# Reordering the prologue of a causal-convolution kernel and giving its last products one block shape

## The chip, the cores and the metric

The kernel runs on one core of a Trainium2 chip. Times are device microseconds (us) of one execution. The profile is one further execution taken by the hardware profiler; its span is about 2 us shorter than the timed number. An execution would count as slow if it took over 1.5% more than the fastest of the same kernel.

In the profile PE is TensorE (matrix products and transposes), PEld its weight load, DVE is VectorE, ACT is ScalarE, POOL is GpSimd and SP is SyncE, which here only issues DMA transfers (SPq is its queue). L727 is line 727 of that kernel's own source file; the changed kernel's file is one line shorter, so L1024 before is L1023 after, and so on.

## The reference

A causal convolution over time (15 taps, 2 tokens apart), a gate, and an output product. x is 2 x 16000 tokens of 144 channels in bfloat16, w is 15 x 144 x 288, w_o is 144 x 144.

```python
def reference(x, w, w_o):
    B, T, D = x.shape
    K = w.shape[0]                      # 15 taps
    dil = 2
    pad = (K - 1) * dil                 # 28
    xp = jnp.pad(x, ((0, 0), (pad, 0), (0, 0)))
    h = jnp.einsum('btc,cd->btd', xp[:, pad:pad + T, :], w[0])
    for i in range(1, K):
        off = pad - i * dil
        h = h + jnp.einsum('btc,cd->btd', xp[:, off:off + T, :], w[i])
    f, g = h[..., :D], h[..., D:]       # (copies cut)
    return (jnp.tanh(f) * _sigmoid(g)) @ w_o
```

## The kernel before

The 32000 tokens are cut into 128 segments of 250, one for each partition. A tile holds one token of every segment, and eight tiles make an "oct". TensorE writes its results to PSUM (PS in the profile), where the program uses eight banks, 0 to 7, and VectorE or ScalarE copies them out (an *eviction*; the two XB evictions of 128x512 together took 1.01 us on VectorE before the change). The program multiplies with the channels on partitions, so every tile is transposed: in the prologue by TensorE itself, later by DMA (XA<-STA in the profile; STA is a staging copy made by VectorE). 128 of the 144 channels are in XA; the other 16, of eight tiles at a time, are in XB.

The first 10 tokens of each segment (the *direct* tiles, k = 0 to 9) are computed plainly: 15 matmuls against the weights WA, tap by tap, and two against WB for the 16 leftover channels. Tap i of tile e reads tile e - 2i, so taps 12 to 14 read the oldest tiles and taps 0 to 3 the newest. The other 240 tokens use a scheme that shares products between tokens. It saves matmuls and costs VectorE work: sums of weights (WC, WS, WT, WV, WD) and differences of tiles (V, DU, DD, GX, GU, GV, GD, BE, BF).

The order of instructions on each engine is fixed when the program is built, by the kernel's own list scheduler. It takes each operation's inputs, its scheduled duration (`dur`) and its `prio`; a `floating` operation may be moved past others on its engine. So a small change to one operation can shift the whole static order.

The prologue, with cuts ("..."):

```python
wa_pieces = [(0, 4), (4, 8), (8, 12), (12, 15)]       # taps of w, loaded in this order, between x's pieces
pro_pieces = [(0, 14), (14, 22), (22, E0), (E0, EP)]  # tiles of x: the oldest first
...
for o in range(-4, 1):                                # input transposes on TensorE (L565)
    b = (o + 4) % 4                                   # PSUM banks 0 to 3
    eng = "act" if o in (-3, -1, 0) else "dve"        # who copies them out of PSUM (L574)
    ...
warm(16)                                              # small matmuls that keep TensorE busy (L541)
...
for o, tiles, bb in ((-1, range(E0 - 4, E0), 7), (0, range(E0, E0 + 8), 5)):   # XB: banks 7 and 5
    ...                                               # 12 transposes (L602)
    g.add("dve", lambda v, ...: v.tensor_copy(XB[...], PSb[...]), ...)         # eviction on VectorE (L606)
...
for b in range(6, 8):                                 # one 288-wide matmul into bank 6, one into bank 7 (L1071)
    g.add("pe", [lambda t: t.matmul(bank(b), lhsT=ID[:], rhs=WARM[:], start=True, ...)], ...)

def direct(k, b, pi, t0, t1, after=None):             # taps t0 to t1 of direct tile k (L727)
    e = H + k
    g.add("pe", region(b, [XA tile e - 2 * i for i in range(t0, t1)], [WA[:, i, :] ...], start=(t0 == 0)),
          floating=k >= KF, prio=2 if k >= KF else 1, ...)        # KF = 6
for pi, (t0, t1) in enumerate(wa_pieces):             # taps 0 to 3 of six tiles, then 4 to 7, ...
    for k in range(6):
        direct(k, db[k], pi, t0, t1)
```

Here `start=True` marks the first matmul of a sum in the program; the later ones are meant to add to it.

The end. The last unit's odd tiles are not transposed by DMA but in four "end pairs": 144 channels are split in 128 + 16, so a 128x128 transpose alternates with a 128x16 one, and a product over 128 rows with one over 16:

```python
def ship_pair(o0, o1, dl):
    ...
    for i in range(2):
        fns.append(transpose(PSb[:, ...],    Z[:, zs[i], dl*D : dl*D+128]))        # L772, 128x128
        fns.append(transpose(PSb[0:DB, ...], Z[:, zs[i], dl*D+128 : dl*D+D]))      # L773, 128x16
    ...
    for i in range(2):
        fns.append(matmul(lhsT=zt(q, 128*i, 128), rhs=WOR[:, 0, :], start=(i == 0)))           # L780
        fns.append(matmul(lhsT=zt(q, 256+128*i, 128)[0:DB, :], rhs=WOR[0:DB, 1, :], start=False))  # L782
    ...                                                                            # ScalarE eviction L786, then stores
```

Of the kernel before, what the change touches and what calls it, by code (L numbers as in the profile page):

```python
# [327 lines left out]
def _conv_wavenet_kernel(nc, x, w, w_o, out):  # L328
# [39 lines left out]
    KF = 6  # L368
    LAG = 2
    SPREAD = 12  # L370
# [3 lines left out]
    with contextlib.ExitStack() as st:  # L374
# [25 lines left out]
        WARM = sb("WARM", [NP, N2], BF16)  # L400
# [94 lines left out]
        for pi, (e0, e1) in enumerate(pro_pieces):  # L495
            if pi:
                t0, t1 = wa_pieces[pi - 1]
                g.add("sp", ld_w(t0, t1), w=[("WA", pi - 1)], dur=0.55, dma="wa", nbytes=(t1 - t0) * 128 * N2 * 2)
            if e0 >= H:
                g.add("sp", ld_x(flat(Xp[:, e0:e1, :]), 0, NP, e0, e1), w=[("Xp", pi, 0), ("Xp", pi, 1)], dur=0.45, dma="xp", nbytes=NP * (e1 - e0) * D * 2)  # L500
                continue
            g.add("sp", ld_x(flat(Xp[1:1 + n16, e0:e1, :]), 1, 1 + n16, e0, e1), w=[("Xp", pi, 0)], dur=0.45, dma="xp", nbytes=n16 * (e1 - e0) * D * 2)
            g.add("sp", ld_x(flat(Xp[1 + n16:NP, e0:e1, :]), 1 + n16, NP, e0, e1), w=[("Xp", pi, 1)], dur=0.45, dma="xp", nbytes=15 * (e1 - e0) * D * 2)
        g.add("act", lambda e: e.dma_start(flat(Xp[0:1, 0:H, :]), bass.AP(x_t, 0, [[L * D, 1], [1, H * D]])), w=[("Xp", 0, 2)], dur=0.5, dma="xp", nbytes=8064)
        g.add("act", lambda e: e.dma_start(flat(Xp[0:1, H:E0, :]), bass.AP(x_t, 0, [[L * D, 1], [1, KD * D]])), w=[("Xp", 2, 2)], dur=0.5, dma="xp", nbytes=576)
        t0, t1 = wa_pieces[3]
        wa_op = g.add("sp", ld_w(t0, t1), w=[("WA", 3)], dur=0.55, dma="wa", nbytes=(t1 - t0) * 128 * N2 * 2)
# [11 lines left out]
        g.add("pool", lambda p: p.memset(WARM[:], 0.0), w=["WARM"], dur=0.3)  # L519
# [36 lines left out]
        for pi in range(4):  # L556
            e0, e1 = pro_pieces[pi]
            for o in range(-4, 1):
# [3 lines left out]
                b = (o + 4) % 4  # L562
# [6 lines left out]
                eng = "act" if o in (-3, -1, 0) else "dve"  # L569
# [7 lines left out]
            warm(16)  # L577
# [20 lines left out]
        for o, tiles, bb in ((-1, range(E0 - 4, E0), 7), (0, range(E0, E0 + 8), 5)):  # L598
            fns = []
            for e in tiles:  # L600
# [5 lines left out]
            g.add("dve", lambda v, o=o, i0=i0, bb=bb: v.tensor_copy(XB[:, bslot(o), i0:8, :].rearrange("p a b -> p (a b)"), PSb[:, bb * 1024 + 128 * i0:bb * 1024 + 1024]),  # L606
                  r=[bk], w=[("XB", bslot(o))], frees=[bk], dur=0.335 if o < 0 else 0.6)
# [156 lines left out]
        def ship_pair(o0, o1, dl):  # L764
# [6 lines left out]
            for i in range(2):  # L771
                fns.append(lambda t, i=i: t.transpose(PSb[:, pa.b * 1024 + 128 * i:pa.b * 1024 + 128 * i + 128], Z[:, zs[i], dl * D:dl * D + 128], ID[:]))  # L772
                fns.append(lambda t, i=i: t.transpose(PSb[0:DB, pb.b * 1024 + 128 * i:pb.b * 1024 + 128 * i + 128], Z[:, zs[i], dl * D + 128:dl * D + D], ID[:]))  # L773
            g.add("pe", fns, r=[("Z", zs[0], dl), ("Z", zs[1], dl), "ID"], alloc=[pa, pb], dur=0.24, floating=True)
            g.add("dve", lambda v: v.tensor_copy(zt(q, 0, 256), PSb[:, pa.b * 1024:pa.b * 1024 + 256]), r=[pa], w=[("ZTL", q, 0), ("Xr", 0)], frees=[pa], dur=0.21, prio=0)
            g.add("act", lambda a: a.activation(zt(q, 256, 256)[0:DB, :], PSb[0:DB, pb.b * 1024:pb.b * 1024 + 256], ACT.Copy), r=[pb], w=[("ZTL", q, 1)], frees=[pb], dur=0.29, prio=0)
            bo = _Bank()
            fns = []
            for i in range(2):
                fns.append(lambda t, i=i: t.matmul(PS[:, bo.b * 512 + i * D:bo.b * 512 + i * D + D], lhsT=zt(q, 128 * i, 128), rhs=WOR[:, 0, :],  # L780
                                                   start=(i == 0), stop=True, skip_group_check=True))
                fns.append(lambda t, i=i: t.matmul(PS[:, bo.b * 512 + i * D:bo.b * 512 + i * D + D], lhsT=zt(q, 256 + 128 * i, 128)[0:DB, :], rhs=WOR[0:DB, 1, :],  # L782
                                                   start=False, stop=True, skip_group_check=True))
# [274 lines left out]
        def direct(k, b, pi, t0, t1, after=None):  # L1058
            e = H + k
            g.add("pe", region(b, [(lambda e_=e - DIL * i: xa_tile(e_)) for i in range(t0, t1)], [(lambda i_=i: WA[:, i_, :]) for i in range(t0, t1)], t0 == 0),  # L1060
                  r=[("XA", aslot(o)) for o in sorted(set(oct_of(e - DIL * i)[0] for i in range(t0, t1)))] + [("WA", pi)], dur=(t1 - t0) * MM, floating=k >= KF, prio=2 if k >= KF else 1, soft=(after,), **({"alloc": [b.bk]} if t0 == 0 and k % 2 == 0 else {"w": [b.bk]}))

# [6 lines left out]
        for b in range(6, 8):  # L1069
            bk = _Bank(b)  # L1070
            g.add("pe", [lambda t, bk=bk: t.matmul(bank(bk.b), lhsT=ID[:], rhs=WARM[:], start=True, stop=True, skip_group_check=True)],  # L1071
                  r=["ID", "WARM"], alloc=[bk], frees=[bk], dur=MM)
# [7 lines left out]
        for pi, (t0, t1) in enumerate(wa_pieces):  # L1080
# [8 lines left out]
        def direct_parts(k):  # L1089
            out = [lambda pi=pi, t0=t0, t1=t1: direct(k, db[k], pi, t0, t1, fin[0] if k >= 8 and t0 == 0 else None) for pi, (t0, t1) in enumerate(wa_pieces)]  # L1090
# [90 lines left out]
        pattern = [(x.rstrip("+"), x.count("+")) for x in PATTERN.split()]  # L1181
# [8 lines left out]
        for t in range(-reach, NUN):  # L1190
# [3 lines left out]
            for name, off in pattern:  # L1194
# [36 lines left out]
        dorder = [x for x, _ in pattern if x[0] == "D"]  # L1231
# [91 lines left out]
```

## Time and profile before

Median 333.14 us (three runs). The span of the profile is 331.2 us.

| engine | busy, of a span of 331.2 us | in the steady part |
|---|---|---|
| TensorE | 323.0 us (98%) | 50.00 of every 50 us |
| VectorE | 302.6 us (91%) | 49.3 of 50 |
| ScalarE | 259.4 us (78%) | 42.9 of 50 |

From the page: the busy times, and the chain of waits (followed back from the last instruction, shares of the span by engine).

```profile
PE 323.0 (98%) x2736; PEld 249.4 (75%) x2736; DVE 302.6 (91%) x662; ACT 259.4 (78%) x626; POOL 17.2 (5%) x30
...
PE 93%; DVE 5%; ACT 1%; issue 1%; POOL 0%; POOLq 0%
```

The table by stretches of the same kernel. Its columns are the stretch and its length, then busy time and number of instructions of PE, PEld, DVE, ACT and POOL, then the granted clock (the share of TensorE's full clock), DMA share and GB/s.

```profile
5.80:14.70 8.90, 7.40 (x119) 6.88 (x116) 7.79 (x27) 3.78 (x6) 6.13 (x11) 1.00 0.88 251
14.70:27.50 12.80, 12.79 (x105) 10.22 (x106) 12.38 (x31) 4.28 (x10) 5.88 (x11) 1.00 0.93 175
35.00:45.00 10.00, 9.68 (x80) 7.50 (x79) 8.19 (x19) 5.65 (x16) 0.00 (x0) 1.00 1.07 205
105.00:155.00 50.00, 50.00 (x421) 38.44 (x419) 49.30 (x105) 42.90 (x106) 0.00 (x0) 1.00 0.70 146
```

TensorE has no gap from 65 to 305 us. The change does not touch that part, so whatever it gains must come before 65 us or after 305 us. The start in the timeline (start, duration, engine, line, operation; in brackets the idle time before it and who ended it):

```profile
14.25 1.01 DVE L606 COPY XB<-PS 128x512 bf16<-128x512 bf16 x2
14.71 0.30 PE L1071 MATMUL PS<-WARM,ID 128*128 128x288 bf16 x1 [1.51 <-DVE XB L606]
14.85 11.19 PE L727 MATMUL PS<-WA,XA 128*128 128x288 bf16 x90
25.87 1.63 PE L727 MATMUL PS<-WB,XB 128*128 128x288 bf16 x12
42.19 1.57 DVE L1024 TENSOR_TENSOR PS<-PS,Xp 128x576 f32<-128x576 f32 x2 [1.78 <-ACT UX L960]
```

The first real matmul (L727) comes at 14.85 us. Until then TensorE only transposes and warms up, and its last wait, 1.51 us, is for VectorE's copy of XB. The direct block ends at 25.87 + 1.63 = 27.50 us. At 42.19 VectorE has waited 1.78 us for ScalarE's copy UX of a matmul result, so there TensorE was what VectorE waited for.

The end, lines of TensorE and SyncE in the timeline (and ScalarE's last eviction):

```profile
320.05 0.22 PE L772 MATMUL PS<-ID,Z 128*128 128x128 bf16 x1
320.20 0.22 PE L773 MATMUL PS<-ID,Z 128*16 128x128 bf16 x1
320.35 0.23 PE L772 MATMUL PS<-ID,Z 128*128 128x128 bf16 x1
...
320.67 0.67 PE L863 MATMUL PS<-WOR,ZT 128*128 128x144 bf16 x8
...
324.61 1.42 SPq L808 DMA_DIRECT2D out_dram<-OS  x2
327.04 0.35 SPq L851 DMA_DIRECT2D out_dram<-OS  x1
327.43 0.42 SPq L799 DMA_DIRECT2D out_dram<-OS  x1
327.70 0.41 ACT L786 ACTIVATE OS<-PS 128x288 bf16<-128x288 f32 x1 [0.28 <-PE PS L782]
327.90 1.32 SPq L808 DMA_DIRECT2D out_dram<-OS  x2
```

Transposes that alternate in shape start 0.15 to 0.16 us apart. Eight projections of one shape take 0.67 us together. SyncE issues its last four stores from 327.04 to 329.22, with 0.05 us between them, after a pause of 1.01 us. The last eviction is done at 328.11.

### The profile page before, as it was taken

To read this page: it belongs to the slowest core of one execution; us is meant where nothing else is said; L and a number is where in the kernel's file an instruction comes from. 1 tells how busy PE (TensorE), PEld (TensorE's weight loads), DVE (VectorE), ACT (ScalarE), POOL (GpSimd) and SP (SyncE) were. 2 spreads that over 40 slices of the span, in tenths; PEclk is the share of its full clock that TensorE was granted. 3 is DMA by queue.
4 is the path that set the end of the run, shared out by engine and by line. 5 is a ranking of instruction groups with operands and counts; after the bars stand their busy time and mean duration, and the time that the engine had idled before them with its cause. 6 is when DMAs were issued, how large, how long until landed. Compare 5 with 4: busy or idle time off the path is not lost.

```text
span 331.2 us, 7123 instructions
## 1 busy us (share of the span) xinstructions
PE 323.0 (98%) x2736; PEld 249.4 (75%) x2736; DVE 302.6 (91%) x662; ACT 259.4 (78%) x626; POOL 17.2 (5%) x30
## 2 busy tenths in 40 slices
PE   7899999999999999999999999999999999999995
PEld 7787867777777777777777777777777777777773
DVE  1999889999999999999999999999999999895682
ACT  3327577979798897979798897979889797787754
POOL 8740000000000000000000000000000000000000
PEclk9999999999999999999999999999999999999997
DMA  8889942928759392956839394874919194411443
GB/s 213 265 124 210 218 121 43 191 84 169 174 99 206 81 207 100 182 158 126 218 63 194 117 177 135 146 200 93 248 38 200 38 154 117 97 48 38 107 109 107
DMA packets 112509, 46.46 MB, mean 140 GB/s; under 512 B 103822, under 2 KB 106303, under 8 KB 112477
## 3 DMA queue, kind: packets, MB, share of 16 engines
q1 hardware_dynamic: 111961, 45.68, 64.6%
q8 instruction: 21, 0.34, 0.4%
q0 software_dynamic: 512, 0.33, 0.4%
q14 instruction: 11, 0.09, 0.1%
q10 hardware_dynamic: 4, 0.01, 0.0%
HBM read 11.82 MB, written 9.22 MB: 64 GB/s over the span
## 4 chain that ended last, share of the span: by engine, by line
PE 93%; DVE 5%; ACT 1%; issue 1%; POOL 0%; POOLq 0%
PE PS L727 81%; PE PS L832 8%; DVE Xp L1012 2%; PE PS L541 1%; DVE WC L616 1%; DVE V L673 1%; DVE PS L1033 0%; PE PS L782 0%; PE PS L863 0%; PE PS L780 0%; PE PS L773 0%; DVE XA L574 0%; PE PS L772 0%; DVE PS L1024 0%; DVE Z L756 0%
## 5 line engine op out<-in xcount | busy, mean ns | idle before, releaser
L1012 DVE TENSOR_TENSOR Xp<-PS,UX 128x576 f32<-128x576 f32 x90 | 65.2, 752 | 7.0 <-PE PS L727 6.4
L1024 DVE TENSOR_TENSOR PS<-PS,Xp 128x576 f32<-128x576 f32 x90 | 68.2, 758 | 3.6 <-ACT UX L960 1.8
L727 PE MATMUL PS<-WA,GD 128*128 128x288 bf16 x360 | 69.8, 286 | 0.3 <-DVE PS L1024 0.3
L748 ACT ACTIVATE TS<-PS 128x288 f16<-128x288 f32 x125 | 51.4, 411 | 14.7 <-PE PS L727 10.0
L891 ACT ACTIVATE PS<-PS 128x288 f32<-128x288 f32 x120 | 45.4, 401 | 17.5 <-PE PS L727 17.5
L751 ACT ACTIVATE TS<-PS 128x288 f16<-128x288 f32 x125 | 50.7, 405 | 0.0
L960 ACT ACTIVATE UX<-PS 128x576 f32<-128x576 f32 x60 | 39.0, 651 | 14.7 <-PE PS L727 13.4
L727 PE MATMUL PS<-WS,GU 128*128 128x288 bf16 x210 | 44.1, 286 | 0.0
L655 ACT ACTIVATE STB<-XBc 128x512 bf16<-128x512 bf16 x60 | 35.9, 630 | 10.0 <-DVE V L673 5.6
L840 ACT ACTIVATE OS<-PS 128x432 bf16<-128x432 f32 (+1 forms) x88 | 42.4, 488 | 0.5
L832 PE MATMUL PS<-WOR,ZT 128*128 128x144 bf16 (+1 forms) x322 | 42.3, 253 | 0.0
L727 PEld LDWEIGHTS PS<-WA,GD 128*128 128x128 bf16 x360 | 34.2, 98 | 10.4 <-DVE PS L1024 0.8
L756 DVE TENSOR_TENSOR Z<-TS 128x288 bf16<-128x288 f16 x125 | 37.3, 300 | 4.0 <-ACT TS L751 3.8
L727 PE MATMUL PS<-WB,XB 128*128 128x288 bf16 x140 | 37.6, 286 | 0.0
L727 PE MATMUL PS<-WB,BF 128*128 128x288 bf16 x120 | 34.3, 286 | 0.0
L727 PE MATMUL PS<-WB,BE 128*128 128x288 bf16 x120 | 34.3, 286 | 0.0
L832 PEld LDWEIGHTS PS<-WOR,ZT 128*128 128x128 bf16 x322 | 28.0, 98 | 6.1 <-ACT OS L840 0.6
L727 PE MATMUL PS<-WD,DD 128*128 128x288 bf16 x180 | 31.9, 286 | 0.2 <-ACT PS L891 0.2
L727 PE MATMUL PS<-WA,DD 128*128 128x288 bf16 x180 | 30.9, 287 | 0.3
L727 PE MATMUL PS<-WC,V 128*128 128x288 bf16 x180 | 30.6, 286 | 0.0
L727 PE MATMUL PS<-WT,DU 128*128 128x288 bf16 x120 | 24.8, 288 | 0.7 <-DVE Xp L1012 0.7
L727 PEld LDWEIGHTS PS<-WS,GU 128*128 128x128 bf16 x210 | 20.2, 98 | 5.7 <-ACT PS L891 0.3
(89 smaller groups left out, 521.2 us busy)
## 6 DMA issues: line engine op xcount, KB each, us to landing
Xr<-in_x_dram SPq DMA_DIRECT2D x15, 576.0 KB, 4.0
out_dram<-OS SPq DMA_DIRECT2D x29, 288.0 KB, 2.8
WA<-in_w_dram SPq DMA_DIRECT2D x3, 288.0 KB, 5.0
ZT<-Z SPq DMA_TRANSPOSE x32, 3.4
Xp<-in_x_dram SPq DMA_DIRECT2D x2, 252.0 KB, 5.3
XA<-STA SPq DMA_TRANSPOSE x30, 3.2
XB<-STB SPq DMA_TRANSPOSE x30, 3.7
Xp<-in_x_dram SPq DMA_DIRECT2D x1, 441.0 KB, 4.0
```

Of the source, the lines that this page charges most:

```text
L541: g.add("pe", [lambda t: t.matmul(PS[:, BANK_O * 512:BANK_O * 512 + 128], lhsT=ID[:], rhs=ONES[:], start=True, stop=True)] * n, r=["ID", " ...
L655: return v.activation(STB[:, q, 4 * h:4 * h + 4, :], src, ACT.Copy)
L727: return lambda t: t.matmul(bank(bk.b), lhsT=lhs(), rhs=rhs(), start=start, stop=True, skip_group_check=True)
L748: return a.activation(TS[:, s, 0, :, :], both(bk, 0, D), ACT.Tanh)
L751: return a.activation(TS[:, s, 1, :, :], both(bk, D, D), ACT.Sigmoid)
L756: return v.tensor_tensor(dst, TS[:, s, 0, :, :], TS[:, s, 1, :, :], ALU.mult)
L832: return t.matmul(PS[:, c0:c0 + n * D], lhsT=ZT[:, zt, blk, :], rhs=WOR[:, wi:wi + n, :].rearrange("p a b -> p (a b)"), start=first, stop= ...
L840: return e.tensor_copy(dst, src) if eng == "dve" else e.activation(dst, src, ACT.Copy)
L891: g.add("act", lambda e: e.activation(bank(bk.b + 1), bank(bk.b), ACT.Copy), w=[bk], dur=t_act(N2), prio=0)
L960: g.add("act", lambda e: e.activation(UX[:, k, u % NU, :, :], both(X, 0, N2), ACT.Copy), r=[X], w=[("UX", k, u % NU)], frees=[X], dur=t_ac ...
L1012: g.add("dve", lambda v, k=k, wi=wi, vb=vb, us=us: v.tensor_tensor(wslot(wi), both(vb, 0, N2), UX[:, k, us, :, :], ALU.add), r=[vb, ("UX", ...
L1024: return v.tensor_tensor(both(d, 0, N2), src, wslot(wi), ALU.add)
```

## The change

The intent has two parts.

- **Start.** Weights arrive with taps 12 to 14 first, and direct tiles begin with those taps, which need only the oldest tiles of x. All transposes of the prologue go into banks 6 and 7, so banks 0 to 5 are free for direct tiles at once. All but one eviction of XA and both of XB go to ScalarE. All direct tiles float. The two 288-wide matmuls into banks 6 and 7 go, and warm-up groups shrink from 16 to 8.
- **End.** The end pairs use overlapping 128x128 blocks: channels dl\*D-112 to dl\*D+16 and dl\*D+16 to dl\*D+144, against output weights that the kernel already holds in that layout for the last tile of an oct (slots 14 and 15 of WOR; slot 14 is zero but for its last 16 rows). One shape throughout.

The diff, cut to its core (an empty `PATTERNS` table, which has no effect, the declared inputs and durations of the end pairs, and repeated terms are cut):

```diff
-    KF = 6
+    KF = 0
+    WARMS = 8
...
-        WARM = sb("WARM", [NP, N2], BF16)
...
-                t0, t1 = wa_pieces[pi - 1]
+                t0, t1 = wa_pieces[4 - pi]
...
-        t0, t1 = wa_pieces[3]
+        t0, t1 = wa_pieces[0]
...
-                b = (o + 4) % 4
+                b = 6 + o % 2
...
-                eng = "act" if o in (-3, -1, 0) else "dve"
+                eng = "dve" if o == -4 else "act"
...
-            warm(16)
+            warm(WARMS)
...
-        for o, tiles, bb in ((-1, range(E0 - 4, E0), 7), (0, range(E0, E0 + 8), 5)):
+        for o, tiles, bb in ((-1, range(E0 - 4, E0), 7), (0, range(E0, E0 + 8), 6)):
...
-            g.add("dve", lambda v, ...: v.tensor_copy(XB[...], PSb[...]), ...)
+            xb_op = g.add("act", lambda v, ...: v.activation(XB[...], PSb[...], ACT.Copy), ...)
...
-            g.add("pe", region(b, ..., t0 == 0), ...)
+            g.add("pe", region(b, ..., t0 == 12), ...)
...
-        for b in range(6, 8):
-            bk = _Bank(b)
-            g.add("pe", [lambda t, bk=bk: t.matmul(bank(bk.b), lhsT=ID[:], rhs=WARM[:], start=True, ...)], ...)
...
-        for pi, (t0, t1) in enumerate(wa_pieces):
+        wa_order = [(3, wa_pieces[3]), (2, wa_pieces[2]), (1, wa_pieces[1]), (0, wa_pieces[0])]
+        for pi, (t0, t1) in wa_order:
...
-            out = [lambda ...: direct(k, ..., fin[0] if k >= 8 and t0 == 0 else None) for pi, (t0, t1) in enumerate(wa_pieces)]
+            out = [lambda ...: direct(k, ..., fin[0] if k >= 8 and t0 == 12 else xb_op if k == 6 and t0 == 12 else None) for pi, (t0, t1) in wa_order]
...
-            for i in range(2):
-                fns.append(transpose(PSb[:, ...], Z[:, zs[i], dl * D:dl * D + 128]))
-                fns.append(transpose(PSb[0:DB, ...], Z[:, zs[i], dl * D + 128:dl * D + D]))
+            for c0, bk in ((dl * D - 112, pa), (dl * D + DB, pb)):
+                for i in range(2):
+                    fns.append(transpose(PSb[:, ...], Z[:, zs[i], c0:c0 + 128]))
...
-                fns.append(matmul(lhsT=zt(q, 128 * i, 128), rhs=WOR[:, 0, :], start=(i == 0)))
-                fns.append(matmul(lhsT=zt(q, 256 + 128 * i, 128)[0:DB, :], rhs=WOR[0:DB, 1, :], start=False))
+                for k in range(2):
+                    fns.append(matmul(lhsT=zt(q, 256 * k + 128 * i, 128), rhs=WOR[:, 14 + k, :], start=(i == 0 and k == 0)))
```

The line with `xb_op` asks the scheduler not to start direct tile 6, the first in banks 6 and 7, before the last eviction of XB starts.

More of the change, by code (lines that the diff above doesn't have):

```diff
@@ L367, in _conv_wavenet_kernel @@
     BANK_O = 6
-    KF = 6
+    KF = 0
+    WARMS = 8
     LAG = 2
+    PATTERNS = {}
     SPREAD = 12
@@ L496, in _conv_wavenet_kernel @@
             if pi:
-                t0, t1 = wa_pieces[pi - 1]
-                g.add("sp", ld_w(t0, t1), w=[("WA", pi - 1)], dur=0.55, dma="wa", nbytes=(t1 - t0) * 128 * N2 * 2)
+                t0, t1 = wa_pieces[4 - pi]
+                g.add("sp", ld_w(t0, t1), w=[("WA", 4 - pi)], dur=0.55, dma="wa", nbytes=(t1 - t0) * 128 * N2 * 2)
             if e0 >= H:
@@ L505, in _conv_wavenet_kernel @@
         g.add("act", lambda e: e.dma_start(flat(Xp[0:1, H:E0, :]), bass.AP(x_t, 0, [[L * D, 1], [1, KD * D]])), w=[("Xp", 2, 2)], dur=0.5, dma="xp", nbytes=576)
-        t0, t1 = wa_pieces[3]
-        wa_op = g.add("sp", ld_w(t0, t1), w=[("WA", 3)], dur=0.55, dma="wa", nbytes=(t1 - t0) * 128 * N2 * 2)
+        t0, t1 = wa_pieces[0]
+        wa_op = g.add("sp", ld_w(t0, t1), w=[("WA", 0)], dur=0.55, dma="wa", nbytes=(t1 - t0) * 128 * N2 * 2)
         xp_keys = [[("Xp", 0, 0), ("Xp", 0, 1), ("Xp", 0, 2)], [("Xp", 1, 0), ("Xp", 1, 1), ("Xp", 0, 2)],
@@ L518, in _conv_wavenet_kernel @@
         g.add("pool", lambda p: p.affine_select(ID[:], ONES[:], [[-1, NP]], ALU.is_equal, 0.0, base=0, channel_multiplier=1), r=["ONES"], w=["ID"], dur=0.3)
-        g.add("pool", lambda p: p.memset(WARM[:], 0.0), w=["WARM"], dur=0.3)
         g.add("pool", lambda p: p.memset(WB[:, 1, :], 0.0), w=[("WB", 1)], dur=0.3)
@@ L605, in _conv_wavenet_kernel @@
             i0 = oct_of(tiles[0])[1]
-            g.add("dve", lambda v, o=o, i0=i0, bb=bb: v.tensor_copy(XB[:, bslot(o), i0:8, :].rearrange("p a b -> p (a b)"), PSb[:, bb * 1024 + 128 * i0:bb * 1024 + 1024]),
-                  r=[bk], w=[("XB", bslot(o))], frees=[bk], dur=0.335 if o < 0 else 0.6)
+            xb_op = g.add("act", lambda v, o=o, i0=i0, bb=bb: v.activation(XB[:, bslot(o), i0:8, :].rearrange("p a b -> p (a b)"), PSb[:, bb * 1024 + 128 * i0:bb * 1024 + 1024], ACT.Copy),
+                  r=[bk], w=[("XB", bslot(o))], frees=[bk], dur=0.5 if o < 0 else 0.92)
         wak = [("WA", i) for i in range(4)]
@@ L770, in ship_pair @@
             fns = []
-            for i in range(2):
-                fns.append(lambda t, i=i: t.transpose(PSb[:, pa.b * 1024 + 128 * i:pa.b * 1024 + 128 * i + 128], Z[:, zs[i], dl * D:dl * D + 128], ID[:]))
-                fns.append(lambda t, i=i: t.transpose(PSb[0:DB, pb.b * 1024 + 128 * i:pb.b * 1024 + 128 * i + 128], Z[:, zs[i], dl * D + 128:dl * D + D], ID[:]))
-            g.add("pe", fns, r=[("Z", zs[0], dl), ("Z", zs[1], dl), "ID"], alloc=[pa, pb], dur=0.24, floating=True)
-            g.add("dve", lambda v: v.tensor_copy(zt(q, 0, 256), PSb[:, pa.b * 1024:pa.b * 1024 + 256]), r=[pa], w=[("ZTL", q, 0), ("Xr", 0)], frees=[pa], dur=0.21, prio=0)
-            g.add("act", lambda a: a.activation(zt(q, 256, 256)[0:DB, :], PSb[0:DB, pb.b * 1024:pb.b * 1024 + 256], ACT.Copy), r=[pb], w=[("ZTL", q, 1)], frees=[pb], dur=0.29, prio=0)
+            for c0, bk in ((dl * D - 112, pa), (dl * D + DB, pb)):
+                for i in range(2):
+                    fns.append(lambda t, i=i, c0=c0, bk=bk: t.transpose(PSb[:, bk.b * 1024 + 128 * i:bk.b * 1024 + 128 * i + 128], Z[:, zs[i], c0:c0 + 128], ID[:]))
+            g.add("pe", fns, r=[("Z", z, d) for z in zs for d in (dl - 1, dl)] + ["ID"], alloc=[pa, pb], dur=0.24, floating=True)
+            g.add("dve", lambda v: v.tensor_copy(zt(q, 0, 256), PSb[:, pa.b * 1024:pa.b * 1024 + 256]), r=[pa], w=[("ZTL", q, 0), ("Xr", 0)], frees=[pa], dur=0.33, prio=0)
+            g.add("act", lambda a: a.activation(zt(q, 256, 256), PSb[:, pb.b * 1024:pb.b * 1024 + 256], ACT.Copy), r=[pb], w=[("ZTL", q, 1)], frees=[pb], dur=0.29, prio=0)
             bo = _Bank()
@@ L779, in ship_pair @@
             for i in range(2):
-                fns.append(lambda t, i=i: t.matmul(PS[:, bo.b * 512 + i * D:bo.b * 512 + i * D + D], lhsT=zt(q, 128 * i, 128), rhs=WOR[:, 0, :],
-                                                   start=(i == 0), stop=True, skip_group_check=True))
-                fns.append(lambda t, i=i: t.matmul(PS[:, bo.b * 512 + i * D:bo.b * 512 + i * D + D], lhsT=zt(q, 256 + 128 * i, 128)[0:DB, :], rhs=WOR[0:DB, 1, :],
-                                                   start=False, stop=True, skip_group_check=True))
+                for k in range(2):
+                    fns.append(lambda t, i=i, k=k: t.matmul(PS[:, bo.b * 512 + i * D:bo.b * 512 + i * D + D], lhsT=zt(q, 256 * k + 128 * i, 128), rhs=WOR[:, 14 + k, :],
+                                                            start=(i == 0 and k == 0), stop=True, skip_group_check=True))
             g.add("pe", fns, r=[("ZTL", q, 0), ("ZTL", q, 1)] + wor_keys, alloc=[bo], dur=0.26, floating=True)
@@ L1059, in direct @@
             e = H + k
-            g.add("pe", region(b, [(lambda e_=e - DIL * i: xa_tile(e_)) for i in range(t0, t1)], [(lambda i_=i: WA[:, i_, :]) for i in range(t0, t1)], t0 == 0),
-                  r=[("XA", aslot(o)) for o in sorted(set(oct_of(e - DIL * i)[0] for i in range(t0, t1)))] + [("WA", pi)], dur=(t1 - t0) * MM, floating=k >= KF, prio=2 if k >= KF else 1, soft=(after,), **({"alloc": [b.bk]} if t0 == 0 and k % 2 == 0 else {"w": [b.bk]}))
+            g.add("pe", region(b, [(lambda e_=e - DIL * i: xa_tile(e_)) for i in range(t0, t1)], [(lambda i_=i: WA[:, i_, :]) for i in range(t0, t1)], t0 == 12),
+                  r=[("XA", aslot(o)) for o in sorted(set(oct_of(e - DIL * i)[0] for i in range(t0, t1)))] + [("WA", pi)], dur=(t1 - t0) * MM, floating=k >= KF, prio=2 if k >= KF else 1, soft=(after,), **({"alloc": [b.bk]} if t0 == 12 and k % 2 == 0 else {"w": [b.bk]}))
         def direct_b(k, b):
@@ L1066, in direct_b @@
                   r=[("XB", bslot(-1)), ("XB", bslot(0)), ("WB", 0), ("WB", 1)], w=[b.bk], floating=k >= KF, prio=2 if k >= KF else 1, dur=2 * MM)
-        for b in range(6, 8):
-            bk = _Bank(b)
-            g.add("pe", [lambda t, bk=bk: t.matmul(bank(bk.b), lhsT=ID[:], rhs=WARM[:], start=True, stop=True, skip_group_check=True)],
-                  r=["ID", "WARM"], alloc=[bk], frees=[bk], dur=MM)
         load_xchunk(0).deps.add(wa_op)
@@ L1089, in direct_parts @@
         def direct_parts(k):
-            out = [lambda pi=pi, t0=t0, t1=t1: direct(k, db[k], pi, t0, t1, fin[0] if k >= 8 and t0 == 0 else None) for pi, (t0, t1) in enumerate(wa_pieces)]
+            out = [lambda pi=pi, t0=t0, t1=t1: direct(k, db[k], pi, t0, t1, fin[0] if k >= 8 and t0 == 12 else xb_op if k == 6 and t0 == 12 else None) for pi, (t0, t1) in wa_order]
             def last():
@@ L1180, in _conv_wavenet_kernel, with pattern_of @@
                 ITEMS["D%d%d" % (k, j)] = lambda u, k=k, j=j: item_D(u, k, j)
-        pattern = [(x.rstrip("+"), x.count("+")) for x in PATTERN.split()]
+        def pattern_of(t):
+            return [(x.rstrip("+"), x.count("+")) for x in PATTERNS.get(t, PATTERN).split()]
+        pattern = pattern_of(None)
         reach = max(o for _, o in pattern)
@@ L1193, in _conv_wavenet_kernel @@
                 step = 0
-            for name, off in pattern:
+            for name, off in pattern_of(t):
                 gate[:] = [op for op in g.ops[-60:] if op.eng == "pe" and not op.floating][-1:]
@@ L1230, in _conv_wavenet_kernel @@
         m, r, o0, o1 = octs(NUN - 1)
-        dorder = [x for x, _ in pattern if x[0] == "D"]
+        dorder = [x for x, _ in pattern_of(NUN - 1) if x[0] == "D"]
         dls = [{"D00": 7, "D01": 5, "D10": 3, "D11": 1}[x] for x in dorder]
```

## The prediction

> **What bounds the kernel now.** A table of busy time by stretch shows TensorE without a gap from 65 to 305 us (50.00 of every 50 us). The chain of waits lies on it for 93%, 81% in the convolution matmuls (one per 0.123 us). VectorE is close behind: 49.3 of 50. The change touches only the start and the end, so it must win there.
>
> **Start, before.** In the timeline x and weight pieces land alternately from 5.05 to about 11.9 us. TensorE does 38 input transposes (0.06 to 0.08 us each), 12 for XB, and fills up with warm-up matmuls (16 take 0.94 us). Direct matmuls start only at 14.72, after a 1.5 us wait for VectorE's XB evictions (14.25 to 15.26, queued behind weight sums), which held banks. The block of 102 ends at 27.4.
>
> **Start, after.** The oldest taps need only the oldest tiles, which arrive first, and now their weights come first too. With XA evicted at 7.4 and 8.3 us, direct work can start near 7.5 to 8.4; banks 0 to 5 are free of transposes. TensorE work left from 8.4: 96 direct matmuls x 0.123 = 11.8, 36 transposes about 2, warm-ups about 1.4: it ends near 23.5, 4 us earlier (estimate from these durations). Not all is gain: the next units need VectorE's differences. VectorE is busy from 6.8 to 40.3 but for 0.4 us (an XA transpose DMA, 25.5), then waits 1.8 us for UX, which waits for TensorE. It loses one XA eviction (0.68) and both XB evictions (1.01). So it can move 1.7 + 1.8 = 3.5 us at best, less where it meets the transposing DMAs of octs 1 and 2 (issued 18.05 to 24.9, behind an x chunk that doesn't move). Direct tiles 6 to 9 (8.3 us) fill part of TensorE's waiting. I expect 2.7 us kept of the 4 (1.5 to 4). ScalarE, 3.8 of 8.9 us busy there, has room for three evictions of 1 us.
>
> **End.** The four last pairs alternate 128x128 and 128x16 (or 16x128) blocks: starts are 0.155 us apart for transposes, 0.165 for matmuls, against 0.06 in runs of one shape (eight projections in 0.67 us). [...] 32 such instructions x 0.1 = 3.2 us of TensorE. The last Z is ready at 324.05 but transposed at 324.73, because TensorE is full; the final matmul is at 327.4, the end at 331.2. After: the last Z comes 0.6 us earlier, transposes follow at once, eviction (0.29) and products follow: the end comes 2.4 us earlier (1.6 to 2.8).
>
> **Sum.** 333.1 - 2.7 - 2.4 = 328.0 us; 8 in 10: 326.0 to 330.2. Over 2% faster (under 326.5): 0.17; within 2%: 0.82; slower by over 2%: 0.01.
>
> **Right or wrong in the profile.** First direct matmul near 8 us; the first WB,XB group ends near 23.5; XB evictions on ScalarE before 15; new TensorE waits on VectorE or DMA between 24 and 60, about 1.4 us above the 1.1 there now; from 65 on as before, shifted by 2.7; transposes and products of the end 0.06 to 0.09 apart.
>
> **What would make it wrong.** VectorE or the transposing DMAs keep their times and TensorE gives the head start back as waits (gain near 2.4); VectorE follows fully (gain near 7); the static order comes out worse, with new gaps in the steady part; late ScalarE evictions hold banks 6 and 7[...].

## The result

The changed kernel takes 328.14 us (327.74 to 328.91, five runs) against 333.17. The ratio is 0.9854, with a 95% interval of 0.9839 to 0.9869: about 4.9 us less. That is clear of the noise, though inside the 2% that counts as "same". A ratio here is the mean time of one kernel's fast runs over that of the other's of the same rounds, so it is not quite the ratio of the medians quoted. Where a gain in us is said to be "by ratio", it is (1 - ratio) x 333.2.

The same two parts of the page after:

```profile
PE 318.3 (98%) x2702; PEld 246.3 (75%) x2702; DVE 301.0 (92%) x659; ACT 261.4 (80%) x629; POOL 17.0 (5%) x29
...
PE 81%; DVE 14%; DMA 2%; ACT 1%; issue 0%; POOL 0%; POOLq 0%
```

And the table by stretches after:

```profile
5.80:14.70 8.90, 8.79 (x113) 7.88 (x111) 7.31 (x25) 4.81 (x9) 5.56 (x9) 1.00 0.86 236
14.70:27.50 12.80, 12.80 (x110) 10.28 (x108) 12.27 (x34) 7.42 (x16) 6.25 (x12) 1.00 1.00 179
35.00:45.00 10.00, 10.00 (x82) 7.54 (x81) 10.00 (x25) 8.03 (x20) 0.00 (x0) 1.00 1.01 204
105.00:155.00 50.00, 50.00 (x417) 38.22 (x416) 49.32 (x106) 43.79 (x107) 0.00 (x0) 1.00 0.72 141
```

Two things changed and one did not. The steady part is as before. From 35 to 45 us VectorE went from 8.19 busy to 10.00 of 10. And the chain of waits, which was TensorE's for 93%, now belongs to VectorE for 14%: in the window up to 70 us it runs almost only through VectorE from 8.5 to 55 us, with one transposing DMA. The start in the timeline:

```profile
7.87 0.53 PE L727 MATMUL PS<-WA,XA 128*128 128x288 bf16 x3
...
14.65 1.51 ACT L606 ACTIVATE XB<-PS 128x512 bf16<-128x512 bf16 x2 [1.12 <-PE PS L602]
14.90 7.51 PE L727 MATMUL PS<-WA,XA 128*128 128x288 bf16 x60
22.25 1.63 PE L727 MATMUL PS<-WB,XB 128*128 128x288 bf16 x12
```

And that DMA in the chain of waits after (start, duration, what):

```profile
20.88 5.26 DMA XA<-STA
```

Direct matmuls start at 7.87 instead of 14.85, and the direct block ends at 22.25 + 1.63 = 23.88, 3.6 us earlier. In the chain VectorE then waits for a transposing DMA that takes 5.26 us, the only long piece between 8.5 and 55 us that is not VectorE's own work. VectorE works through most of it and is idle for 0.50 us in the timeline:

```profile
26.16 0.43 DVE L636 COPY STA<-Xr 128x1024 bf16<-128x1024 bf16 x1 [0.50 <-DMA XA<-STA]
```

The end in the timeline:

```profile
316.74 0.39 PE L773 MATMUL PS<-ID,Z 128*128 128x128 bf16 x4
...
319.35 0.66 PE L781 MATMUL PS<-WOR,Xr 128*128 128x144 bf16 x8
...
320.40 1.43 SPq L807 DMA_DIRECT2D out_dram<-OS  x2
321.47 0.78 ACT L785 ACTIVATE OS<-PS 128x288 bf16<-128x288 f32 x2
321.87 0.61 SPq L850 DMA_DIRECT2D out_dram<-OS  x1
322.53 0.42 SPq L798 DMA_DIRECT2D out_dram<-OS  x1
323.00 1.32 SPq L807 DMA_DIRECT2D out_dram<-OS  x2
```

Four transposes now take 0.39 us. SyncE's last four stores still follow each other within 0.05 us, now from 321.87 to 324.32, but without the pause ahead of them: the issues at 320.40 end at 321.83. So the four begin only 0.38 us ahead of the end of the last eviction (322.25), where it was 1.07 us before (327.04 against 328.11), and they take 2.45 us instead of 2.18.

**Splitting the gain.** A common mark in both traces is the group of 15 projections that starts the final phase (PS<-WOR,ZT x15). It starts at 315.20 before and at 311.89 after: 3.3 us of gain lie before it. From it to the end of the span is 16.0 us before and 14.4 after: 1.6 us lie behind it. The prediction had put 2.7 and 2.4 there.

### The profile page after: what moved, and what is told of

The parts are those of the page before. It is cut to its first block, busy times and chain, and to the rows that moved or that the text cites. A ratio compares the mean times of both kernels' runs of the same rounds, so it can differ in the third digit from the quotient of the medians.

```text
span 326.3 us, 7055 instructions
## 1 busy us (share of the span) xinstructions
PE 318.3 (98%) x2702; PEld 246.3 (75%) x2702; DVE 301.0 (92%) x659; ACT 261.4 (80%) x629; POOL 17.0 (5%) x29
## 4 chain that ended last, share of the span: by engine, by line
PE 81%; DVE 14%; DMA 2%; ACT 1%; issue 0%; POOL 0%; POOLq 0%
PE PS L727 71%; PE PS L831 8%; DVE Xp L1011 2%; DMA XA<-STA 2%; DVE V L673 2%; PE PS L541 1%; DVE PS L1023 1%; DVE DD L673 1%; DVE STA L636 1%; DVE DU L673 1%; DVE Z L756 1%; DVE PS L1032 1%; DVE GD L673 1%; DVE WC L616 1%; DVE GU L673 1%
## 5 line engine op out<-in xcount | busy, mean ns | idle before, releaser
L831 PE MATMUL PS<-WOR,ZT 128*128 128x144 bf16 (+1 forms) x322 | 42.3, 253 | 0.0
L831 PEld LDWEIGHTS PS<-WOR,ZT 128*128 128x128 bf16 x322 | 28.0, 98 | 6.1 <-ACT OS L839 0.6
```

The lines of the kernel that those rows point to most:

```text
L831: return t.matmul(PS[:, c0:c0 + n * D], lhsT=ZT[:, zt, blk, :], rhs=WOR[:, wi:wi + n, :].rearrange("p a b -> p (a b)"), start=first, stop= ...
```

## The experiments

The theory was, as in the prediction: (a) start and end are separate gains, and add; (b) the start gain is as large as VectorE can follow; (c) the early order of the taps makes the start possible; (d) the end gain is in the switches of block shape. The rivals: for (b), that TensorE's own work is the limit, so that any TensorE work removed counts; for (c), that freeing banks and moving evictions to ScalarE suffice; for (d), that small blocks are slow as such. A further question came with the result: where did 0.8 of the predicted 2.4 us at the end go? All times, in order of the text. The mark is the start of the run of 15 projections near the end (L832 before, L831 after) in the profiled execution:

| run | median us (lowest to highest, runs) | ratio to before, 95% interval | mark, us | mark to end, us |
|---|---|---|---|---|
| before | 333.17 (332.87 to 333.61, 5) | 1 | 315.20 | 16.0 |
| after | 328.14 (327.74 to 328.91, 5) | 0.9854 (0.9839 to 0.9869) | 311.89 | 14.4 |
| start_only | 329.63 (329.34 to 330.52, 5) | 0.9897 (0.9882 to 0.9912) | 311.67 | 16.0 |
| end_only | 331.33 (330.98 to 331.55, 5) | 0.9943 (0.9929 to 0.9957) | 314.87 | 14.4 |
| end_grouped | 332.04 (331.57 to 332.56, 6) | 0.9965 (0.9951 to 0.9979) | 314.80 | 14.8 |
| old_order (wrong result) | 329.74 (329.25 to 330.51, 5) | 0.9898 (0.9884 to 0.9913) | 313.23 | 14.5 |
| old_order_marked | 331.35 (331.05 to 331.95, 6) | 0.9945 (0.9930 to 0.9960) | 314.94 | 14.5 |
| xb_dve | 331.68 (330.17 to 332.42, 6) | 0.9949 (0.9930 to 0.9969) | 315.39 | 14.4 |
| ws_pool | 334.59 (334.32 to 335.18, 5) | 1.0043 (1.0031 to 1.0056) | 318.45 | 14.45 |
| dve_load | 329.52 (328.96 to 330.08, 5) | 0.9885 (0.9867 to 0.9902) | 313.47 | 14.4 |
| warm0 | 327.65 (326.88 to 328.15, 5) | 0.9837 (0.9825 to 0.9850) | 310.74 | 14.5 |
| act_stores | 328.37 (327.83 to 328.72, 4) | 0.9854 (0.9838 to 0.9869) | 311.95 | 14.75 |
| early_store | 328.15 (327.43 to 329.33, 5) | 0.9851 (0.9830 to 0.9873) | 311.30 | 14.3 |
| best_b | 328.22 (327.68 to 329.15, 4) | 0.9852 (0.9831 to 0.9873) | 311.23 | 14.4 |

The kernel before, run again beside each set, had medians of 333.20 to 333.27. The three sets of experiments ran on different chips, so runs of different sets are compared by ratio. A mark comes from one profiled execution, a ratio from all runs; they agree in size, not to a tenth. One reason is seen in the traces: VectorE's first copy (XA<-PS) starts at 6.80 us before and after, but at 5.75 in end_only, 5.76 in old_order_marked and warm0, 5.92 in xb_dve and 6.00 in early_store, although the 40 warm-up matmuls ahead of it are the same. So a mark, or the end of the direct block, can be up to 1 us early by luck.

### Each half alone

start_only is the changed kernel with the old end pairs; end_only is the kernel before with the new ones.

```diff
 # start_only: the changed kernel, with
-            for c0, bk in ((dl * D - 112, pa), (dl * D + DB, pb)):   # 128x128 blocks
+            ...                                                       # the old 128x128 / 128x16 pairs
 # end_only: the kernel before, with the opposite edit
```

> The changed kernel with the old end pairs. Marks in the two traces (the 15 projections near the end: 315.20 us before, 311.89 after) put the gain of the start at 3.3 us. If start and end are independent: 333.2 - 3.3 = 329.9 us, and those projections at 311.9. Rival, the start's gain is partly eaten at the end or the end's smaller gain comes from the new start: over 330.5 or under 329.3.

> The kernel before with only the 128x128 end pairs. What is left of the 4.9 us of span after the 3.3 of the start is 1.6 us: 331.6 us (331.2 to 331.9). Rival, my forecast of 2.4 us for the end was right and the new start costs it something: 330.8 us. The last matmul should come 4 us before the end, but the last store's issue should wait for the two store issues ahead of it on SyncE.

By ratio start_only gains 3.43 us and end_only 1.90; their sum, 5.3, is close to the 4.9 of both together. Each of the three intervals is about 0.5 us wide to either side, so the difference is within the noise, and the ratios alone would not show an interaction under about 1 us. The marks say the same: 3.5 us before the mark in start_only with 16.0 behind it as before; 14.4 us behind the mark in end_only, as after. So the two halves are separate, and (a) holds. The prediction's sum was right with two terms that were each off by 0.5 to 0.8 us in opposite directions.

### The end: is it the shape, or the switch of shape?

end_grouped keeps the small blocks of the kernel before and only puts equal shapes side by side: big, big, small, small.

```diff
-                fns.append(lambda t, i=i: t.transpose(PSb[:, ...], Z[:, zs[i], dl * D:dl * D + 128], ID[:]))
+                fns.insert(i, lambda t, i=i: t.transpose(PSb[:, ...], Z[:, zs[i], dl * D:dl * D + 128], ID[:]))
 # and the same for the 128-row products
```

> The kernel before, its end pairs unchanged in shapes but issued as big, big, small, small instead of alternating. If the 0.155 to 0.165 us between starts is paid at each switch of shape: within a group of one shape 0.06 us, at a switch still about 0.155; half of TensorE's loss is gone, 0.6 to 1.0 us faster than before. Rival, each small block costs 0.155 by itself: small to small stays near 0.155 and the time is within 0.3 us of before.

It gains 1.17 us by ratio, a little over the range expected. Its timeline, TensorE's lines:

```profile
319.64 0.28 PE L772 MATMUL PS<-ID,Z 128*128 128x128 bf16 x2
319.84 0.28 PE L773 MATMUL PS<-ID,Z 128*16 128x128 bf16 x2
320.05 0.67 PE L863 MATMUL PS<-WOR,ZT 128*128 128x144 bf16 x8
```

Two transposes of one shape take 0.28 us, of which 0.22 is the length of one: they start 0.06 apart, the small ones too. From group to group it is 0.20 and 0.21, so each switch costs 0.14 to 0.15 from start to start where a non-switch costs 0.06. The small blocks themselves are not slow; (d) holds. The spacings give the switch a number: about 0.09 us more each.

### The start: what the order of the taps carries

old_order is the changed kernel with the taps, and the weights' loads, in the order of before.

```diff
-        wa_order = [(3, wa_pieces[3]), (2, wa_pieces[2]), (1, wa_pieces[1]), (0, wa_pieces[0])]
+        wa_order = list(enumerate(wa_pieces))
 # loads: wa_pieces[pi - 1], piece 3 last; start flag: t0 == 0 instead of t0 == 12
```

> The changed kernel, but weights loaded and direct tiles begun with the newest taps, as before; evictions on ScalarE, banks and end kept. If the early start of the direct matmuls carries the gain of the start: they can't begin before the last XA eviction (13.5 us), their block of 102 ends near 27 instead of 23.9, and most of the 3.4 us goes: 330.3 to 331.3 us. Rival, the relief of VectorE alone (1.7 us of evictions) carries it: under 329.8 us.

Its result was wrong, with a relative error of 0.0868. That was not intended, and its cause is worth more than its time. A simulation of the program's values put the error in two tiles (tokens 22 and 24 of each segment), in all partitions. The program's instruction list shows what is different there: in this order the first 288-wide matmul into bank 7 after the transposes is an *accumulating* one (WS,GU, without the start flag), meant to add to a value that ScalarE had copied into the bank. In the kernel before, a WS,GU matmul is the first to accumulate in bank 7 as well; ahead of it stands one of the two 288-wide matmuls of zeros into banks 6 and 7, which look like warm-up. The changed kernel removed them; in its order the direct tiles 6 and 7, with a start flag, happen to be first in those banks, and its result is right. So the missing matmul was my suspect. What it leaves in the bank no trace or run shows.

old_order_marked puts the two matmuls back into old_order.

```diff
+        for b in range(6, 8):
+            bk = _Bank(b)
+            g.add("pe", [lambda t, bk=bk: t.matmul(bank(bk.b), lhsT=ID[:], rhs=WARM[:], start=True, ...)], ...)
```

> The run with the old order of taps and weights gave two wrong tiles of 250 (tokens 22 and 24 of each segment). My explanation: with that order a unit of the main part is the first to accumulate in bank 7[...]; the kernel before had one matmul into each of banks 6 and 7 there, which the change removed. With these two put back: a correct result (error near 0.009), and the same time as without, 329.3 to 330.2 us, which is 1.6 us of the start's 3.4 lost. Rival: still wrong.

The result is right. In its instruction list the WS,GU matmul still follows the put-back one directly in bank 7, so it is that matmul, and not a different order, that mends the result; this confirms that its absence was the cause. Why the WS,GU matmul needs it was not shown. The time is not what I expected: 331.35. By ratio none of the start gain is left (0.9945, where end_only has 0.9943), and by the mark 0.3 us (315.20 against 314.94). Its timeline:

```profile
15.95 0.41 PE L1072 MATMUL PS<-WARM,ID 128*128 128x288 bf16 x2
...
44.65 0.31 DVE L758 TENSOR_TENSOR Z<-TS 128x288 bf16<-128x288 f16 x1 [3.15 <-ACT TS L753]
```

In the stretch from 5.80 to 14.70 TensorE is busy only 6.51 of 8.90 us, and later VectorE waits 3.15 us at 44.65 for a result that ScalarE gives it late. The direct block ends at 25.87 in old_order and at 26.15 in old_order_marked, against 23.88 after and 27.50 before. So the order of the taps is worth about 2 us or more at the end of the direct block (the trace of old_order_marked has the early start named above). How much of the kept 3.3 us it carries I can only bracket: 1.3 us by the mark and 1.5 by ratio in old_order (which computes a wrong result, with the same work), 3.0 by both in old_order_marked, whose static order also differs elsewhere. The 329.74 of old_order missed my expectation (330.3 to 331.3) and lies at the edge of what I had given to the rival (under 329.8). In neither run did freeing the banks and moving the evictions give all of it, as the rival to (c) would have it; the exact share stays open.

### The start: moving the XB evictions

xb_dve is the changed kernel with the XB evictions back on VectorE.

```diff
-            xb_op = g.add("act", lambda v, ...: v.activation(XB[...], PSb[...], ACT.Copy), ..., dur=0.5 if o < 0 else 0.92)
+            xb_op = g.add("dve", lambda v, ...: v.tensor_copy(XB[...], PSb[...]), ..., dur=0.335 if o < 0 else 0.6)
```

> The changed kernel with both XB evictions (1.01 us together) back on VectorE. The chain of waits of the changed kernel runs through VectorE from 8 to 55 us. If that is right, their time comes back in full: 328.1 + 0.7 to 1.1 = 328.8 to 329.2 us, seen as a shift of the first stretch without TensorE waits. Rival, TensorE's matmul block bounds the start: within 0.3 us of the changed kernel.

It took 331.68, far over what one us of VectorE work explains: 0.9949 against 0.9854 is 3.2 us. The order changed with it. From the timelines of ScalarE, VectorE and TensorE:

```profile
23.98 1.15 ACT L655 ACTIVATE STB<-XBc 128x512 bf16<-128x512 bf16 x2 [5.47 <-DMA XB<-STB]
25.75 0.31 DVE L756 TENSOR_TENSOR Z<-TS 128x288 bf16<-128x288 f16 x1 [2.72 <-ACT TS L751]
28.21 0.42 PE L727 MATMUL PS<-WT,DU 128*128 128x288 bf16 x2 [2.27 <-DVE DU L673]
28.47 1.91 PE L727 MATMUL PS<-WA,XA 128*128 128x288 bf16 x8
```

ScalarE sat 5.47 us behind a staging copy whose buffer a DMA held, with its gate evaluations (TS) queued behind. VectorE waited 2.72 us for TS, so the difference DU came late, and TensorE had a gap of 2.27 us. Then eight matmuls took 1.91 us: they start about 0.24 apart, where 0.123 is usual. The table by stretches gives the granted clock just after the gap (third number from the right):

```profile
28.80:29.50 0.70, 0.70 (x5) 0.44 (x4) 0.70 (x3) 0.70 (x2) 0.00 (x0) 0.50 0.94 182
```

It is 1.00 up to 28.6, then 0.50 from about 28.7 to 32.1. So this run does not tell what the eviction alone is worth; it shows that one static order away lies a stall, and that a stall of 2.27 us was followed by about 3.4 us at half clock (in TensorE's timeline the matmuls start about 0.24 us apart until 32.09, and 0.12 from there). Of the gaps in the two runs that follow, that of 4.91 us was followed by 0.50 as well (ws_pool), while that of 1.50 us left the clock at 1.00 (dve_load). One case each; whether it is the length of the gap that decides, no run here shows.

### The start: weight sums on GpSimd

ws_pool tried for more: move the WS sums of weights from VectorE to the idle GpSimd.

```diff
-             ... [("WA", i)], [("WS", i)], 0.4 if n == 2 else 0.25)
+             ... [("WA", i)], [("WS", i), "PQ"], 1.2 if n == 2 else 0.7, "pool")   # "PQ" orders it against GpSimd's other work
```

> The changed kernel with the four pair sums of weights (WS, 0.37 us each on VectorE, 1.4 together) on the idle GpSimd. If VectorE bounds the start and can follow: 1.0 to 1.4 us faster than the changed kernel, 326.8 to 327.2 us. If the wait for the XA transpose at 20.9 to 26.2 us bounds it instead: VectorE waits longer there and the gain is under 0.5 us. If both engines' accesses get in each other's way, VectorE's sums and differences become longer than 0.37 and 0.60 us and it is slower.

It lost: 1.0043, slower than the kernel before and 6.3 us slower than the changed kernel by ratio. From the timeline:

```profile
12.08 1.38 DVE L616 TENSOR_TENSOR WC<-WC 128x288 bf16<-128x288 bf16 x1
13.56 2.28 DVE L673 TENSOR_TENSOR V<-XA 128x1024 bf16<-128x1024 bf16 x1
14.00 1.28 POOL L616 TENSOR_TENSOR WS<-WA 128x576 bf16<-128x576 bf16 x1
...
29.17 0.66 PE L727 MATMUL PS<-WT,DU 128*128 128x288 bf16 x2 [4.91 <-ACT TS L751]
```

While a GpSimd addition runs, the VectorE operation beside it takes 2.28 us instead of 0.69, or 1.38 instead of 0.30: longer by 1.59 and 1.08 us, where the GpSimd additions beside them last 1.28 and 1.33 (the profiler's spans on GpSimd are rough). Beside each of the four additions VectorE's operation ends 0.16 to 0.56 us after GpSimd's, and two of the four VectorE operations, that at 13.56 among them, started first. How the two engines come to hinder each other the trace does not show. A 128x576 addition takes 0.45 us on VectorE and took 1.28 to 1.33 on GpSimd, 2.9 times (any hindrance included), so VectorE lost more by each than it was relieved of. TensorE then waited 4.91 us, and its granted clock was 0.50 in every stretch that I read from 28.3 to 32.5 us (0.56 on average from 27.5 to 35); the twelve matmuls from 29.62 to 32.50 start 0.24 us apart. Its 6.3 us show in these two places; how they divide was not tested.

### The start: does VectorE bound it?

dve_load adds 0.88 us of useless VectorE work in the middle of the weight sums (four additions), without telling the scheduler, so every engine's order is that of the changed kernel.

```diff
+            g.ops[-1].fns.insert(0, lambda v, j=j: v.tensor_tensor(OS[...], WC[:, 1, 2, :], WC[:, 1, 3, :], ALU.add))   # x4
```

> The changed kernel with four needless sums of 128x288 (0.22 us each, 0.88 together) on VectorE at 15.6 us; every engine's order is otherwise that of the changed kernel, so this is VectorE's load alone, without the changed order that spoiled the run with the XB evictions on VectorE. If VectorE bounds the start: 0.6 to 0.9 us slower than the changed kernel, 328.7 to 329.0 us, and no TensorE gap over 1 us. Rival, TensorE or the loads bound it: under 0.3 us slower.

The four additions take their time at 16.13, and TensorE has a new gap in the timeline:

```profile
16.13 0.96 DVE L1121 TENSOR_TENSOR OS<-WC 128x288 bf16<-128x288 bf16 x4
25.21 0.43 DVE L636 COPY STA<-Xr 128x1024 bf16<-128x1024 bf16 x1 [1.01 <-DMA XA<-STA]
26.85 0.42 PE L727 MATMUL PS<-WT,DU 128*128 128x288 bf16 x2 [1.50 <-DVE DU L673]
```

By ratio it is 1.03 us slower than the changed kernel (0.6 to 0.9 expected; the two intervals just touch, but its fastest run, 328.96, is slower than the changed kernel's slowest, 328.91), by the mark 1.6. The mark's 1.6 can be followed in VectorE's timeline, operation by operation: it is 0.31 us late before the load, by a wait for ScalarE's first eviction; 1.2 after it; and 1.58 once it is past the transposing DMAs of XA, for which it waits 1.01 us at 25.21 and no longer 0.50 us at the next one. From there on nothing is made up. So the added VectorE time comes out at the end: VectorE bounds the start of the changed kernel, with that DMA in its chain. TensorE's gap was larger than I had expected. It left the clock at 1.00 (in the stretches 14.7 to 27.5 and 28.8 to 29.5 us).

### The start: does TensorE bound it?

warm0 drops the four groups of eight warm-ups in the prologue, about 1.9 us of TensorE time (32 at 0.058) before 15 us.

```diff
-            warm(WARMS)
```

> The changed kernel without the 32 warm-up matmuls between the input transposes (the 40 at the very start stay). TensorE is relieved of about 1.8 us. If VectorE bounds the start: within 0.4 us of the changed kernel, 327.8 to 328.5, and TensorE's waits on others before 60 us grow by what was taken away. Rival, TensorE bounds it: 326.3 to 327 us. [...]

It gains 0.57 us by ratio, between what I had given to VectorE (within 0.4) and to the rival (1.1 to 1.8), and its interval (0.9825 to 0.9850) overlaps that of the changed kernel (0.9839 to 0.9869). TensorE's waits before 65 us grow from about 1.25 to about 2.8 us: most of what TensorE saves it hands back as waits. The mean granted clock of its profiled execution was 1.00. Against 0.88 us of VectorE work that cost all of itself, 1.9 us of TensorE work gave under a third. That speaks for (b) against its rival. One caution: in the profile of warm0 the first 40 warm-ups took 3.71 us, against 4.45 in those of before and after, with the same code. The mark of 310.74 contains that luck, and it is nearly all of the gain there: VectorE's first copy starts 1.04 us earlier, the direct block ends 2.4 us earlier (21.44), and the mark comes 1.15 us earlier. It is VectorE's start that the mark follows, not the end of TensorE's block.

### The end: where 0.8 us went

In the kernel before, the last eviction ends 12.91 us after the mark (327.70 + 0.41 - 315.20), after the change 10.36 (322.25 - 311.89): 2.55 us earlier, as predicted (2.4). But the last store's issue ends 14.02 us after the mark before (329.22 - 315.20) and 12.43 after (324.32 - 311.89): 1.59 earlier. So 0.95 us was given back between the last eviction and the end of the last issue: the four issues begin 0.69 us later against the last eviction, because their first data come later against it and SyncE is still busy with two other issues, and they take 0.27 us longer. In the six traces that I read for it, with all stores on SyncE (before, after, start_only, end_only, end_grouped, early_store) the span ends 1.97 to 2.02 us after that last issue ends, so SyncE's queue looked like the limit.

Three runs tried to take it back. act_stores issues the last two pairs of stores from ScalarE; early_store evicts the last projections sooner so that SyncE can begin its stores earlier; best_b is both, without the warm-up groups and with 32 instead of 40 first warm-ups.

```diff
 # act_stores
-            g.add("sp", f, ..., dma="st", ...)
+            g.add(eng, f, ..., dma="st" if eng == "sp" else "sta", ...)     # store_both(o0, o1, dl, "act") for the last two
 # early_store
-                       ..., prio=2 if last else 1)
+                       ..., prio=2 if last else 0 if o >= 2 * NPAIR - 3 and gi == 2 else 1)
 # best_b: both, and
-            warm(WARMS)
-        warm(40)
+        warm(32)
```

> The changed kernel with its last two stores issued from ScalarE, all other instructions in the same order. If the end is now bound by the issue of four stores one after another on SyncE (last one issued at 323.66 though its data were ready at 322.25): the last issue ends near 323.5, 0.6 to 1.0 us faster than the changed kernel, about 327.3 us. Rival, the time from data to end is the landing of the stores, whichever queue issues them: no change, 328.1.

> The changed kernel with one ScalarE eviction near the end (the last third of the last 288 KB row of outputs) moved ahead of three others, and its store with it; nothing else changes place. In six traces the span ends 4.2 to 4.8 us after that store is issued, whatever the last stores do. If the draining of these stores bounds the end: issue at about 320.5 to 321 instead of 321.9, and 0.5 to 1.0 us faster than the changed kernel, 327.1 to 327.6 us. Rival, the last evictions and stores bound it: no change, or 0.3 us slower for the later evictions.

> A version meant to beat both: the changed kernel with the early store, the last two stores from ScalarE, no warm-ups between the transposes, and 32 instead of 40 at the very start, since the chain of waits begins with them to 5.8 us and the first x piece has landed at 5.1 to 5.4. If the gains add: 327.65 (no warm-ups between) less 0.6 for the end and 0.3 for the start, 326.8 us (326.3 to 327.4). [...]

None moved the time. In early_store SyncE is already full before the last eviction (from its queue in the timeline):

```profile
319.80 0.34 SPq L850 DMA_DIRECT2D out_dram<-OS  x1
320.19 1.43 SPq L807 DMA_DIRECT2D out_dram<-OS  x2
321.66 0.61 SPq L798 DMA_DIRECT2D out_dram<-OS  x1
322.32 1.31 SPq L807 DMA_DIRECT2D out_dram<-OS  x2
```

From 319.80 to 323.63 its issues follow each other within 0.05 us, so a store moved forward frees nothing; the last issue ends 12.33 us after the mark instead of 12.43. I had expected more and was wrong. In act_stores and best_b the last issue does end 0.7 to 1.0 us earlier relative to the mark, but the span then ends 2.7 to 3.3 us after it, instead of 2.0, and so where it did. In the table by stretches of half a microsecond the DMA traffic stops by 325.5 us after the change (0.8 before the end of the span) and by 325.0 in early_store (0.6), but by 325.5 in act_stores (1.2) and by 324.5 in best_b (1.1). So it is not simply that the transfers ran longer: something behind them ends these two runs later. SyncE's queue is where the 0.95 us lies in time, but taking the issues off it won nothing back, so the queue is not shown to be the cause. What sets the end stays open.

### What did not reach the chip, and a better version

Two builds were mended before any run: the first ws_pool had a race between two GpSimd operations, and the first act_stores deadlocked in its order, with stores on two queues sharing semaphores; in the run ScalarE's stores have their own ("sta"). No version beat the changed kernel outside the intervals. warm0 comes nearest, at 327.65 us.

## Why the prediction was right

The time, 328.14 against 328.0 predicted, is right. The terms of the sum are less so.

- **What bounds the kernel:** right. TensorE has no gap in the steady part before or after, and the gain is all in the start and the end, as start_only and end_only show by adding up.
- **Direct matmuls near 8 us, first WB,XB group done near 23.5:** 7.87 and 23.88. The block came 3.6 us earlier, not 4.
- **XB evictions on ScalarE before 15:** they ran from 14.65 to 16.16, after the predicted time but harmlessly: no instruction waited for them in the trace, since banks 6 and 7 are wanted only at about 23.7.
- **2.7 of the 4 us kept, with 1.4 us of new TensorE waits:** the step that failed. The waits did not come. TensorE was idle 1.10 us between 27.5 and 65 us before, and 1.15 us after. 3.3 to 3.5 us were kept. VectorE followed as far as I had said it could "at best", 3.5 us: it lost the evictions, and its 1.78 us wait at 42.19 is gone (10.00 of 10 us busy from 35 to 45). What I had taken off for the transposing DMAs was not lost: VectorE waited 0.50 us for one of them after, 0.42 before.
- **VectorE limits the start:** right, and shown directly. 0.88 us of VectorE work cost 1.0; 1.9 us of TensorE work less gave 0.57. The chain of waits agrees: VectorE's share went from 5% to 14%.
- **Switches of shape cost the time at the end:** right. The spacings are 0.06 in one shape and 0.14 to 0.17 across a switch; the 128x16 transposes start 0.06 apart like the 128x128 ones when grouped (end_grouped).
- **The end 2.4 us earlier:** over-sized. The last eviction did come 2.55 us earlier, but I followed the chain only to that eviction and took "the end" to follow. Behind it stand SyncE's store issues, six without a pause where it was two and four; 0.95 us lies between the last eviction and the end of the last issue, and 1.6 was kept. Moving the issues did not bring it back, so why the end keeps no more stays open.
- **What it did not see at all:** that without the two matmuls removed as warm-up the result is wrong in the old order of the taps (relative error 0.0868 in old_order, right with them put back in old_order_marked), so that the order became a condition of correctness.

The two wrong terms, -0.7 and +0.8 us, cancelled. That the total is right to 0.1 us is luck, and no proof of its terms.

## What to carry to other kernels

When a change gives one engine a head start, find the engine that must follow it, and add up how much that one can move; test it by adding a known load to it, and by removing some from the other, rather than by the share of busy time. When an end is shortened, follow the chain to the last DMA landing: the issues of the stores may close up, and part of the gain can be lost behind the last computation (here 0.95 us). Test whether they are the limit before calling them so; here moving them changed nothing (328.37 us in act_stores against 328.14). Before a seemingly idle matmul is deleted, check the result in every order of instructions that you try: here the same deletion gave a right result in one order and a relative error of 0.0868 in another. And keep matmuls of equal block shape together: here 0.06 us from start to start within a shape, 0.14 to 0.17 across a switch.
